# Talking-heads attention with a bilinear MoE: six q times k of a chunk begun one unit later, and loads of k, v, x and weights at other units

## The chip, the cores and the metric

One core of one Trainium2 chip runs the whole program. The metric is device time in microseconds (us), the median of several executions; in a profiled execution the span from the core's first to its last instruction is also known.

## The reference

```python
scores = scale * np.matmul(q, k.transpose(0, 1, 3, 2))        # batch 4, heads 12, seq 448, dim 64
scores = np.einsum('bhij,hg->bgij', scores, w_pre)            # heads are mixed
scores = scores - np.max(scores, axis=-1, keepdims=True)
attn = np.exp(scores)
attn = attn / (np.sum(attn, axis=-1, keepdims=True) + 1e-09)
attn = np.einsum('bhij,hg->bgij', attn, w_post)               # and mixed again
x = np.matmul(attn, v)                                        # then laid out as 1792 x 768
a, b = x @ w_a, x @ w_b                                       # 768 -> 1536
out = (a * b) @ w_out                                         # 1536 -> 768
```

## The kernel before

Attention runs first, the MoE after it. A batch has 448 queries, cut into four chunks of 120, 120, 120 and 88, and each chunk into units of 20 queries (the last of a batch has 8). That makes 16 chunks and 92 units, 23 to a batch. The main loop runs over the units s, and everything is written out in the order in which each engine gets it; there is no scheduler behind it.

For a whole chunk, six calls of `qk(c, i)` multiply q by k for two heads each, into one PSUM tile of two banks, `pst`, of which there is one. The result is copied to the scores `s` in SBUF, by ACT for i = 0 and 3 (`i % OWN == 0`), by DVE for the others. There are two tiles of `s`, so chunk c writes where chunk c - 2 was. `gather(u)`, four DMAs issued by POOL (`sb<-s`), brings the rows of a unit into `sb`, with all heads of a few queries side by side. It is issued AH = 4 units before use, and the first of a chunk only once all six `qk` have been issued.

A unit s then does this: `premix(s)` (PE: `mp<-sb,wp`, heads mixed); `evac_p(s - 2)` (ACT: `pt<-pp`); `smax(s)` (DVE: `nm`, the row maximum; ACT: `a`, the exponential with its row sum); the items of the table `items`, that is `qk` of a coming chunk and `av` (PE: `xp<-pt,v`, attention times v, at odd units of a batch mostly, one or two calls); `norm(s)` (DVE: `rs`, `rc`, `kr`); `postmix(s - 1)` (PE: `pp<-kr,a`, the second mixing and a transposition). Of two `qk` in one unit, the second is issued after `postmix`; such a unit is said to have a pair. At the end of a unit stand loads of k and q (table `after`).

In `items`, chunk c's six `qk` begin at the unit a = starts[c - 1] - 4 and are spread evenly up to starts[c] - 5; starts[c] is the chunk's first unit. Counted in the batch, that is units 2 to 7 for the second chunk, 8 to 13 for the third, 14 (a pair) to 18 for the next batch's first, 19 to 22, 0 and 1 for its second. Chunk 1 has a table of its own.

Loads are issued by SP. Batch 0's v comes in 12 pieces, two a unit, from unit V_FIRST; the next batch's v comes one piece a unit from unit V_AT of a batch on; the next batch's six pieces of k every other unit from K_AT. At unit `last_prep + 1` (83) the tiles of q and k are given up, and the first two blocks of MoE weights (`raw`, three pieces each) and the six parts of x (`xhl`) are loaded; `tail` is the work that splits them, a few steps a unit.

Of the kernel before, what the change touches and what calls it, by code (L numbers as in the profile page):

```python
# [21 lines left out]
def talking_heads_bilinear_kernel(  # L22
# [12 lines left out]
    B, _, G, S = k.shape  # L35
# [26 lines left out]
    WARM = 40  # L62
    WARM3 = 60
    Q1E = 3
    V_AT = 8
    V_FIRST = 1
    V_PIECES = 12
    K_AT = 3
    OWN = 3
    LQ = 4  # L70
    scale = 1.0 / float(D) ** 0.5
# [2 lines left out]
    for b in range(B):  # L74
        t0 = 0
        while t0 < S:
            n = min(CHUNK, S - t0)
# [8 lines left out]
    NUB = NU // B  # L86
# [40 lines left out]
    def later(fn, n=3):  # L127
        todo_at.setdefault(now[0] + n, []).append(fn)
# [62 lines left out]
    def load_v(b, i):  # L191
        g, i = divmod(i, V_PIECES // 2)
        e, i = divmod(i, V_PIECES // 4)
        n = H // 2 // (V_PIECES // 4)
        rows, heads = slice(64 * e, 64 * e + C), slice(n * i, n * i + n)
        nc.sync.dma_start(out=vt[b % 2][g][rows, heads], in_=v[b, g][C * e:C * e + C, heads])
# [199 lines left out]
    items, after, ready = {}, {}, {}  # L396
    starts = [u for u in range(NU) if units[u][1] == 0] + [NU]
    qk_at = {}
    for c in range(1, NC):
        b, t0, _ = chunks[c]  # L400
        a, e = max(starts[c - 1] - AH, 0), starts[c] - AH
        for i in range(G):
            at_s = qk_at[c, i] = i * Q1E // G if c == 1 else a + i * (e - a) // G
            items.setdefault(at_s, []).append((qk, c, i))
            if t0 == 0:
                after.setdefault((b - 1) * NUB + K_AT + 2 * i, []).append((load_k, b, i))
        ready[c] = qk_at[c, G - 1]
        for j in range(G // QG):
            if c > 1:
                when = max(qk_at[c, QG * j] - LQ, 0)  # L410
                after.setdefault(when, []).insert(0, (load_q, c, j))
            if c > 1 or j:
                after.setdefault(max(qk_at[c, QG * j] - 1, 0), []).append((spread_q, c, j))
    last_prep = ready[NC - 1]
    for a in range(NA - 1):
        b, u0, n = groups[a]
# [6 lines left out]
    def open_moe():  # L423
        short.close()
        mo["c"] = ctx.enter_context(tc.tile_pool(name="mc", bufs=2))
        mo["w"] = ctx.enter_context(tc.tile_pool(name="mw", bufs=2))
# [16 lines left out]
    def load_raw(u, parts=1):  # L443
        kind, i, e = u
        t = mo["c"].tile([128, CW, 2], I32, tag="raw", name="raw")
        to, src = t.rearrange("p (k f) t -> p k (f t)", k=KD), (w_ab if kind == "f" else w_out)[i, e].bitcast(I32)
        n = KD // parts
        raws[u] = t
        return [
            lambda k=k: nc.sync.dma_start(out=to[:, k:k + n], in_=src[:, k:k + n]) for k in range(0, KD, n)  # L450
        ]
# [166 lines left out]
    with tc.manual_schedule():  # L618
# [30 lines left out]
        for s in range(NU + 2):  # L649
            now[0] = s  # L650
            if s == last_prep + 1:
                open_moe()
                pieces = load_raw(order[0], 3) + load_raw(order[1], 3)
                pieces += [lambda i=i: load_x(0, (i,)) for i in range(KD)]
                for i, fn in enumerate(pieces):
                    fn() if i < 3 else later(fn, (i - 1) // 2)
                tail = tail_ops()
            if s == NU - 2:
                load_x(1)
            if s == NU - 1:  # L660
                load_x(2)
            while nxt_g <= min(s + AH, NU - 1) and ready.get(units[nxt_g][0], -1) < s:
                gather(nxt_g)
                nxt_g += 1
            b, i = divmod(s, NUB)
            if 0 <= s - V_FIRST < V_PIECES // 2:
                for p in range(2):
                    load_v(0, 2 * (s - V_FIRST) + p)
            if b + 1 < B and 0 <= i - V_AT < V_PIECES:
                load_v(b + 1, i - V_AT)  # L670
            for fn in todo_at.pop(s, ()):
                fn()
            if s < NU:
                premix(s)
            if 2 <= s <= NU:
                evac_p(s - 2)
            if s < NU:
                for k_ in blocks_of(s):
                    smax(k_)
            pairs = [it for it in items.get(s, ()) if it[0] is qk]  # L680
            for it in items.get(s, ()):
                if it not in pairs[1:]:
                    it[0](*it[1:])
            if s < NU:
                norm(s)
            if 0 <= s - 1 < NU:
                postmix(s - 1)
            for it in pairs[1:]:
                it[0](*it[1:])
            for it in after.get(s, ()):  # L690
                it[0](*it[1:])
            if s >= last_prep + 2:
                take(tail, RATE if s < NU - LATE else RATE2)
            if s == NU:
                for _ in tail:
                    pass
                tail = split_ops(1)
                evac_p(NU - 1)
                run_a(0, 0)
            if s == NU + 1:  # L700
                run_b(0, 0)
# [59 lines left out]
        for j in range(B * KD):  # L761
            b, m = divmod(j, KD)
# [57 lines left out]
```

## Time and profile before

| | |
|---|---|
| median of 3 runs | 927.26 us (924.5 to 930.05) |
| the profiled execution | 927.72 us, of which its span is 926.0 us |
| mean granted clock of TensorE | 0.983 of full speed |
| PE busy | 881.8 us, 95% of the span |
| DVE, ACT, POOL busy | 520.6, 365.6, 444.7 us |
| DMA, mean over the span | 159 GB/s |

The difference of 1.7 us between the execution and its span lies before the first and behind the last instruction. Attention takes about the first 382 us. The busy share of PE is a mean over that part, in which it waits at times, and the MoE, in which it hardly ever does.

### The profile page before, as it was taken

The page shows a single profiled execution, that of the slowest core. Times are in us where ns is not written, and L with a number is a line of the kernel's source. Part 1 is how long each engine was busy: PE and PEld are TensorE (multiplying, and loading weights), DVE is VectorE, ACT ScalarE, POOL GpSimd, SP SyncE. Part 2 cuts the span into 40 slices and gives each one's busy share as a digit, 9 for nine tenths or more (in the row PEclk, how much of TensorE's full clock was granted, in tenths as well). Part 3 has the DMA queues.
Part 4 walks back from the last instruction along what each step waited for, and adds up shares of the span by engine and source line. Part 5 has one row for each costly group of instructions (what it writes and reads, how often), then busy time and mean ns, then how long its engine had stood idle before and what let it go on. Part 6 is the DMA issues. An engine that isn't in the chain of part 4 may idle for free.

```text
span 926.0 us, 26343 instructions
## 1 busy us (share of the span) xinstructions
PE 881.8 (95%) x11092; PEld 709.0 (77%) x11092; DVE 520.6 (56%) x899; ACT 365.6 (39%) x841; POOL 444.7 (48%) x551
## 2 busy tenths in 40 slices
PE   7879998899899997899999999999999999999998
PEld 4445665566566664788999999999999989999997
DVE  4656776767667767477755755557455445151500
ACT  1556676667656775522111111111111244343531
POOL 7466676766757764033333322233232245554552
PEclk9789999999999998999999999999999999999999
DMA  5598667855966567543533333342342664746441
GB/s 157 163 200 173 172 178 182 198 157 163 217 148 172 163 173 190 183 140 123 167 119 145 108 137 128 116 149 98 118 147 92 233 231 148 256 132 252 132 146 60
DMA packets 78647, 147.40 MB, mean 159 GB/s; under 512 B 29342, under 2 KB 58122, under 8 KB 77506
## 3 DMA queue, kind: packets, MB, share of 16 engines
q1 hardware_dynamic: 50402, 108.05, 36.4%
q0 software_dynamic: 28128, 37.68, 16.2%
q8 instruction: 87, 1.43, 0.7%
q14 instruction: 30, 0.25, 0.1%
HBM read 80.23 MB, written 26.74 MB: 116 GB/s over the span
## 4 chain that ended last, share of the span: by engine, by line
PE 70%; POOL 7%; DMA 7%; DVE 6%; issue 6%; ACT 3%; SPq 0%; ACTq 0%; DVEq 0%; POOLq 0%
PE po L510 6%; PE po L511 6%; PE po L509 6%; PE pa L509 6%; PE pa L511 6%; PE pb L511 6%; PE pa L510 6%; PE pb L509 6%; PE pb L510 6%; POOL sb L285 5%; DMA sb<-s 5%; PE xp L384 4%; PE pst L241 4%; PE pp L348 4%; PE mp L305 4%
## 5 line engine op out<-in xcount | busy, mean ns | idle before, releaser
L285 POOL DMA_DIRECT2D sb<-s x350 | 201.3, 584 | 105.3 <-PE mp L305 30.1
L471 POOL TENSOR_TENSOR cvm<-cvm,cvr 128x768 int32<-128x768 int32 x36 | 66.9, 1858 | 224.3 <-DVE cvm L470 219.2
L499 POOL TENSOR_TENSOR wl<-rawo,wh 128x768 fp32r<-128x768 f32 x48 | 93.2, 1962 | 105.2 <-ACT wh L498 105.2
L315 DVE TENSOR_REDUCE nm<-mp 124x1 f32<-124x448 f32 x180 | 104.0, 617 | 69.0 <-PE mp L305 63.5
L318 ACT ACTIVATE a<-mp,nm 124x448 f32<-124x448 f32 x180 | 112.9, 634 | 70.6 <-DVE nm L315 70.5
L348 PEld LDWEIGHTS pp<-kr,a 60*56 60x56 f32 (+1 forms) x5760 | 98.0, 129 | 45.1 <-issue 29.7
L521 ACT COPY sa<-pa 128x448 f32<-128x448 f32 x48 | 25.6, 533 | 232.7 <-PE pa L511 171.2
L241 PE MATMUL pst<-k,q 64*64 64x448 f32 (+1 forms) x744 | 100.7, 580 | 16.0 <-ACT s L268 11.8
L348 PE MATMUL pp<-kr,a 60*56 60x60 f32 (+1 forms) x5760 | 102.1, 217 | 14.4 <-issue 10.7
L363 ACT COPY pt<-pp 120x480 f32<-120x480 f32 x176 | 91.1, 576 | 53.9 <-PE pp L348 53.5
L305 PE MATMUL mp<-sb,wp 60*64 60x448 f32 x720 | 102.9, 565 | 5.3 <-DMA sb<-s 2.6
L510 PE MATMUL pa<-xhl,wh 128*128 128x448 f32 x288 | 104.8, 364 | 1.7 <-DVE xhl L439 1.7
L510 PE MATMUL po<-hl,wh 128*128 128x448 f32 x288 | 105.8, 367 | 0.6 <-DVE hl L546 0.6
L509 PE MATMUL pa<-xhl,wh 128*128 128x448 f32 x288 | 106.0, 368 | 0.0
L511 PE MATMUL pa<-xhl,wl 128*128 128x448 f32 x288 | 105.9, 368 | 0.0
L511 PE MATMUL po<-hh,wl 128*128 128x448 f32 x288 | 105.8, 368 | 0.0
L509 PE MATMUL po<-hh,wh 128*128 128x448 f32 x288 | 105.1, 365 | 0.0
L511 PE MATMUL pb<-xhl,wl 128*128 128x448 f32 x282 | 103.8, 368 | 0.7 <-POOL wl L499 0.7
L531 DVE TENSOR_TENSOR hf<-pb,sa 128x448 f32<-128x448 f32 x47 | 29.3, 624 | 133.4 <-PE pb L511 123.7
L509 PE MATMUL pb<-xhl,wh 128*128 128x448 f32 x282 | 103.6, 367 | 0.0
L510 PE MATMUL pb<-xhl,wh 128*128 128x448 f32 x282 | 102.4, 363 | 0.0
L546 DVE TENSOR_TENSOR hl<-hl,hh 128x448 fp32r<-128x448 f32 x48 | 57.3, 1248 | 78.5 <-ACT hh L545 78.5
(74 smaller groups left out, 1343.0 us busy)
## 6 DMA issues: line engine op xcount, KB each, us to landing
sb<-s POOLq DMA_DIRECT2D x346, 105.0 KB, 4.6
rawo<-wod SPq DMA_DIRECT2D x24, 768.0 KB
raw<-in_w_ab_dram SPq DMA_DIRECT2D x22, 768.0 KB
hd<-hf SPq DMA_DIRECT2D x48, 224.0 KB
raw<-in_w_out_dram SPq DMA_DIRECT2D x12, 768.0 KB
k<-in_k_dram SPq DMA_DIRECT2D x24, 224.0 KB
v<-in_v_dram SPq DMA_DIRECT2D x48, 112.0 KB
xhl<-xd SPq DMA_DIRECT2D x24, 224.0 KB
```

The source lines that it names most:

```text
L241: nc.tensor.matmul(out[64 * e:64 * e + cols.stop - cols.start], lhsT=qt[c, i // QG][rows, i % QG, cols], rhs=kt[b, i][rows],)
L285: (nc.sync if u <= AH and i % 2 else nc.gpsimd).dma_start(out=sbt[u][i % 2][r:r + m * H], in_=rows)
L305: nc.tensor.matmul(mt[u, i // 2][col:col + M], lhsT=wp[r:r + m, :M], rhs=tiles[i % 2][r:r + m])
L315: nc.vector.tensor_reduce(nm[:m], mp[:m], axis=AXX, op=ALU.max, negate=True)
L318: nc.scalar.activation(a[:m], mp[:m], ACTF.Exp, bias=nm[:m], scale=1.0, accum_out=rss[u][:m, j:j + 1])
L348: nc.tensor.matmul(pp_t[i][64 * e:64 * e + C, H * r:H * r + H, j, :m], lhsT=a[rows, keys:keys + C], rhs=kr[rows, j, :, :m],)
L363: nc.scalar.copy(to[:C2, :, o + QB * i:o + QB * i + QB], pp_t[i][:C2].rearrange("p x j t -> p x (j t)"))
L471: lambda: nc.gpsimd.tensor_tensor(m, m, r, op=ALU.add),
L499: nc.gpsimd.tensor_tensor(ll[:, sl], raw, hh.bitcast(F32)[:, sl], op=ALU.subtract)
L509: nc.tensor.matmul(o, lhsT=hh[:, k0 + kk], rhs=mh[:, kk], start=(kk == 0), stop=False)
L510: nc.tensor.matmul(o, lhsT=hh[:, k0 + kk], rhs=ml[:, kk], start=False, stop=False)
L511: nc.tensor.matmul(o, lhsT=ll[:, k0 + kk], rhs=mh[:, kk], start=False, stop=(kk == n - 1))
```

## The change

The starts of `qk` move: a chunk with six units gets its six `qk` at a + 1, a + 2, a + 3 (two), a + 4, a + 5, one with five units (the next batch's first) at a + 1, a + 2 (two), a + 3, a + 4 (two). So the last one stays at its unit. In a batch the second chunk's are now at units 3, 4, 5 (two), 6, 7, the third's at 9, 10, 11 (two), 12, 13, the next batch's first at 15, 16 (two), 17, 18 (two), its second's at 20, 21, 22 (two), 0, 1. Units 2, 8, 14 and 19 have none. Loads of k and v get a table of units each; batch 0's v starts one unit later; the MoE's first loads get a table too, and the tail's steps begin one unit later.

```diff
@@ -62,10 +62,11 @@
     WARM = 40
     WARM3 = 60
     Q1E = 3
-    V_AT = 8
-    V_FIRST = 1
+    V_FIRST = 2
     V_PIECES = 12
-    K_AT = 3
+    V_UNITS = (8, 11, 13, 15, 15, 17, 17, 19, 19, 21, 21, 22)
+    K_UNITS = (2, 3, 6, 9, 10, 14)
+    M_UNITS = (0, 0, 1, 1, 2, 3, 3, 4, 4, 5, 5, 5)
     OWN = 3
     LQ = 4
     scale = 1.0 / float(D) ** 0.5
@@ -400,10 +401,10 @@
         b, t0, _ = chunks[c]
         a, e = max(starts[c - 1] - AH, 0), starts[c] - AH
         for i in range(G):
-            at_s = qk_at[c, i] = i * Q1E // G if c == 1 else a + i * (e - a) // G
+            at_s = qk_at[c, i] = i * Q1E // G if c == 1 else a + 1 + (i * (e - a - 1) + 2) // G
             items.setdefault(at_s, []).append((qk, c, i))
             if t0 == 0:
-                after.setdefault((b - 1) * NUB + K_AT + 2 * i, []).append((load_k, b, i))
+                after.setdefault((b - 1) * NUB + K_UNITS[i], []).append((load_k, b, i))
         ready[c] = qk_at[c, G - 1]
         for j in range(G // QG):
             if c > 1:
@@ -652,8 +653,8 @@
                 open_moe()
                 pieces = load_raw(order[0], 3) + load_raw(order[1], 3)
                 pieces += [lambda i=i: load_x(0, (i,)) for i in range(KD)]
-                for i, fn in enumerate(pieces):
-                    fn() if i < 3 else later(fn, (i - 1) // 2)
+                for fn, n in zip(pieces, M_UNITS):
+                    later(fn, n)
                 tail = tail_ops()
             if s == NU - 2:
                 load_x(1)
@@ -666,8 +667,9 @@
             if 0 <= s - V_FIRST < V_PIECES // 2:
                 for p in range(2):
                     load_v(0, 2 * (s - V_FIRST) + p)
-            if b + 1 < B and 0 <= i - V_AT < V_PIECES:
-                load_v(b + 1, i - V_AT)
+            for p in range(V_PIECES):
+                if b + 1 < B and i == V_UNITS[p]:
+                    load_v(b + 1, p)
             for fn in todo_at.pop(s, ()):
                 fn()
             if s < NU:
@@ -689,7 +691,7 @@
                 it[0](*it[1:])
             for it in after.get(s, ()):
                 it[0](*it[1:])
-            if s >= last_prep + 2:
+            if s >= last_prep + 3:
                 take(tail, RATE if s < NU - LATE else RATE2)
             if s == NU:
                 for _ in tail:
```

DVE, batch 0, from unit 14 on, before: `nm` opens a unit, `rs`, `rc`, `kr` are its `norm`, each `COPY s<-pst` evicts one q times k (unit 14's first is ACT's).

```order
L315 TENSOR_REDUCE nm<-mp 124x1 x2
L328 TENSOR_SCALAR rs<-rs 124x2
L329 RECIPROCAL rc<-rs 124x2
L331 TENSOR_TENSOR kr<-kf,rc 124x120
L266 COPY s<-pst 124x2x448
L315 TENSOR_REDUCE nm<-mp 124x1 x2
L266 COPY s<-pst 124x2x448
```

Two units further, in the changed kernel, from unit 16 on:

```order
L316 TENSOR_REDUCE nm<-mp 124x1 x2
L267 COPY s<-pst 124x2x448
L329 TENSOR_SCALAR rs<-rs 124x2
L330 RECIPROCAL rc<-rs 124x2
L332 TENSOR_TENSOR kr<-kf,rc 124x120
L267 COPY s<-pst 124x2x448
L316 TENSOR_REDUCE nm<-mp 124x1 x2
```

The pair has gone from unit 14, where ACT evicted its first half, to unit 16, where DVE evicts both, one ahead of `norm` and one behind it.

ACT, batch 1, units 2 and 3, before: `a` is the exponential of a unit, `pt` the eviction of postmix two units back, `s<-pst` the eviction of the chunk's first q times k.

```order
L318 ACTIVATE a,rs<-mp,nm 124x448 x2
L268 COPY s<-pst 124x2x448
L363 COPY pt<-pp_101 120x48x10
L363 COPY pt<-pp_102 120x48x10
L318 ACTIVATE a,rs<-mp,nm 124x448 x2
```

The same place in the changed kernel:

```order
L319 ACTIVATE a,rs<-mp,nm 124x448 x2
L364 COPY pt<-pp_101 120x48x10
L364 COPY pt<-pp_102 120x48x10
L319 ACTIVATE a,rs<-mp,nm 124x448 x2
L269 COPY s<-pst 124x2x448
```

The eviction of q times k has moved from behind unit 2's exponentials to behind unit 3's.

SP, batch 1, from unit 9's load of k on, before: `paced` is a small write that each unit issues when its first maximum is there, so the rows between two of them belong to the end of one unit and the start of the next.

```order
L203 DMA k<-in_k_dram 128x448
L196 DMA v_103<-in_v_dram 56x512
L199 DMA paced<-nm 1x1
L210 DMA qraw<-in_q_dram 128x360
L196 DMA v_103<-in_v_dram 56x512
L199 DMA paced<-nm 1x1
L203 DMA k<-in_k_dram 128x448
L196 DMA v_103<-in_v_dram 56x512
L394 DMA xd_85<-xs 128x3x160
```

From unit 9's load of k on in the changed kernel:

```order
L204 DMA k<-in_k_dram 128x448
L200 DMA paced<-nm 1x1
L204 DMA k<-in_k_dram 128x448
L197 DMA v_103<-in_v_dram 56x512
L200 DMA paced<-nm 1x1
L211 DMA qraw<-in_q_dram 128x360
L395 DMA xd_85<-xs 128x3x160
L200 DMA paced<-nm 1x1
L197 DMA v_103<-in_v_dram 56x512
```

Before, units 9 to 12 hold two loads of k and three of v; now k stands at the ends of units 9 and 10, and v in units 11 and 13.

## Rows read from the trace of the kernel before

**Rows 1.** Stretches: length, busy time by engine, PE clock, DMA share, GB/s.

```profile
56.52:84.33 27.81, 24.91 (x579) 15.94 (x574) 15.47 (x35) 15.47 (x38) 18.48 (x38) 0.88 0.80 185
...
146.84:170.23 23.39, 21.50 (x577) 14.46 (x568) 15.70 (x39) 15.53 (x38) 16.59 (x32) 1.00 0.87 216
170.23:203.82 33.59, 31.21 (x834) 20.20 (x826) 22.05 (x49) 22.56 (x55) 22.34 (x41) 1.00 0.68 166
232.25:258.16 25.91, 23.19 (x577) 15.07 (x568) 15.85 (x39) 15.64 (x38) 17.87 (x36) 0.93 0.98 214
...
319.40:341.28 21.88, 21.45 (x576) 14.42 (x568) 15.68 (x39) 15.40 (x38) 15.95 (x31) 1.00 0.55 170
341.28:381.62 40.34, 32.11 (x804) 20.42 (x792) 28.93 (x65) 25.18 (x62) 17.37 (x20) 0.92 0.74 196
```

**Rows 2.** Waits of PE in 17 to 382 us: total, times, longest.

```profile
PE pst L241 <- ACT s L268: 11.5, 15, 2.5
PE pp L348 <- issue: 10.7, 7, 2.9
```

**Rows 3.** Timeline of PE, batch 0, units 9 and 10: start, us, instruction, [idle].

```profile
60.90 0.54 PE L305 MATMUL mp<-sb,wp 60*64 60x448 f32 x1
...
64.35 1.77 PE L241 MATMUL pst<-k,q 64*64 64x448 f32 x8 [2.46 <-ACT s L268]
...
70.03 0.94 PE L305 MATMUL mp<-sb,wp 60*64 60x448 f32 x8
```

**Rows 4.** Timeline of ACT at the same place.

```profile
63.39 0.91 ACT L268 COPY s<-pst 107x896 f32<-107x896 f32 x1 [3.73 <-DMA sb<-s]
```

**Rows 5.** Timeline of PE, batch 0, units 2 and 3.

```profile
36.96 1.76 PE L241 MATMUL pst<-k,q 64*64 64x448 f32 x8 [1.31 <-DVE s L266]
38.47 1.74 PE L305 MATMUL mp<-sb,wp 60*64 60x448 f32 x8
```

**Rows 6.** Timeline of PE, batch 1, units 14 to 22.

```profile
170.23 0.94 PE L305 MATMUL mp<-sb,wp 60*64 60x448 f32 x8
...
174.24 0.98 PE L241 MATMUL pst<-k,q 64*64 64x448 f32 x8 [1.48 <-ACT s L268]
175.04 0.93 PE L305 MATMUL mp<-sb,wp 60*64 60x448 f32 x8
176.44 0.98 PE L241 MATMUL pst<-k,q 64*64 64x448 f32 x8 [0.46 <-DVE s L266]
...
181.82 1.16 PE L305 MATMUL mp<-sb,wp 60*64 60x448 f32 x8
183.41 0.98 PE L241 MATMUL pst<-k,q 64*64 64x448 f32 x8 [0.43 <-ACT s L268]
...
187.56 0.94 PE L305 MATMUL mp<-sb,wp 60*64 60x448 f32 x8
...
194.12 0.94 PE L305 MATMUL mp<-sb,wp 60*64 60x448 f32 x8
...
196.47 1.16 PE L305 MATMUL mp<-sb,wp 60*64 60x448 f32 x8
...
201.53 0.55 PE L305 MATMUL mp<-sb,wp 60*64 60x448 f32 x2
```

**Rows 7.** Timeline of DVE, batch 1, unit 14.

```profile
171.27 1.16 DVE L315 TENSOR_REDUCE nm<-mp 124x1 f32<-124x448 f32 x2 [1.77 <-PE mp L305]
```

**Rows 8.** Timeline of ACT, batch 1, unit 14.

```profile
173.28 0.91 ACT L268 COPY s<-pst 124x896 f32<-124x896 f32 x1
```

**Rows 9.** Timeline of PE, batch 3, units 14 to 16.

```profile
341.28 0.94 PE L305 MATMUL mp<-sb,wp 60*64 60x448 f32 x8
...
343.43 0.56 PE L305 MATMUL mp<-sb,wp 60*64 60x448 f32 x1
...
351.43 0.86 PE L348 MATMUL pp<-kr,a 60*56 60x60 f32 x24 [2.85 <-issue]
```

**Rows 10.** Timeline of PE, batch 2, unit 12.

```profile
251.53 0.27 PE L348 MATMUL pp<-kr,a 60*56 60x60 f32 x3 [1.91 <-issue]
```

## Prediction

> **What bounds the kernel now.** I read the stretches first, cut at the premix matmul that opens a unit; i is a unit's number in its batch, 0 to 22. TensorE (PE) is the engine that is nearly always busy: in the undisturbed stretch for units 8 to 13 of the last batch it works 21.45 of 21.88 us. The same six units take 27.81, 23.39 and 25.91 us in the three batches before, where the DMA share is 0.80 to 0.98 instead of 0.55 and in two of them the clock is below 1.00 [rows 1]. So some 11.5 us (5.9, 1.5 and 4.0) are lost there, the only large losses between the start and the last nine units. Units 14 to 22 show none: 31.21 of 33.59 us at a share of 0.68.
>
> The waits of PE come next. Besides waits for the eviction of q times k (ACT alone 11.5 us), seven waits of pp, 10.7 us, are put down to "issue": PE waited for nothing that the profile shows [rows 2]. The longest, 2.85 us, lies in the last stretch, at a share of 0.74 and a clock of 0.92 [rows 1, 9].
>
> The timeline at the start of batch 0's last chunk shows what the first edit is about. ACT idles 3.73 us for a gather that still reads the old scores (sb<-s) and evicts at 63.39 [rows 4]. The next unit's q times k needs the one PSUM tile pst, so PE waits 2.46 us and then runs its eight matmuls at half speed (1.77 us for 0.98), and the unit from 60.90 to 70.03 takes 9.13 us [rows 3]. A unit of the same kind, with a double attention-times-v, takes 5.06 (196.47 to 201.53) [rows 6].
>
> **The change, part by part.** No instruction is added or taken away. What a q times k costs depends on the unit that it stands in, and units alternate: even ones have no attention times v, odd ones a single or double one. Prices from PE's starts:
> - an even unit with one q times k: 2.35 (194.12 to 196.47) [rows 6]; without one: 2.15 (341.28 to 343.43) [rows 9], since postmix, its eviction and the next postmix still follow each other. Taking one away returns 0.2, not its 0.9 of matmul.
> - an even unit with a pair: 4.81 (170.23 to 175.04), 1.48 of it the wait for the first eviction, and 0.46 more in the next unit for the second [rows 6]. ACT began that first eviction only at 173.28, behind its exponentials [rows 8]; DVE would be free after its reduces, at 172.43 [rows 7], 0.8 sooner. So a pair with DVE first is 4.1, or +1.75 over one.
> - an odd unit is PE's own pace: one more q times k is +0.9, and the next unit gets about 0.5 more, since ACT evicts it ahead of the postmix result (no row shows this; between 0 and the 0.98 of matmul and 0.9 of eviction, I take the 0.46 of [rows 6]).
> - after an even unit whose q times k ACT evicts, the next pays 0.43; with a double attention times v it is 5.74 (181.82 to 187.56) instead of 5.06: 0.7 [rows 6].
>
> *The later start.* Units 2 to 13: 2 and 8 lose their q times k (-0.2 each), 3 and 9 lose the ACT stall (-0.4, -0.7), 5 and 11 take a pair (+0.9 each), 6 and 12 follow it (+0.5 each): +1.3 a batch, +3.9 for three. Batch 0 has no attention times v in unit 5, so its pair is of the even kind: 1.75 + 0.5 - 0.2 + 0.9 + 0.5 = +3.45; its units 2, 3 and 9 are priced below. Units 14 to 22 and the next 0 (three times): 14 loses its pair, 4.81 to 2.15, -2.65; 15 loses 0.46 of stall; 16 and 18 get pairs with DVE first, +1.75 each; 17 keeps a stall, -0.3; 19 loses its one, -0.75 (0.9 less a little of the 2.15 effect); 21 gets the 0.7; 22, with only eight queries, takes a pair at +1.3 (between the 0.9 of matmul and 1.75), 0 the +0.5. Together +1.85, +5.6 for three. In all **+13.0 us**. Its ends are 6 (pairs at their matmuls alone) and 19 (every new even pair as dear as the ACT one, +2.46).
>
> What the move takes away: in unit 2 of batch 0 the third q times k waits 1.31 and starts at 36.96; without it the next premix, at 38.47, could start at 35.65 [rows 5]: **-2.8**. Unit 9 of batch 0 falls from 9.13 to 5.06: **-4.1**. The gather that ended that wait landed at about 63.3 [rows 4]; with q times k one unit later, ACT comes to this eviction at about that time, so the wait is covered. If unit 2's gain brings PE there earlier, the gather, which is queued behind the same premixes, comes earlier too, or up to 2.8 of the wait stays.
>
> *The loads.* Six pieces of v and three of k lie in units 8 to 13 now, three and two after. By their shapes a piece of k has 128 x 448 x 4 bytes = 224 KB and one of v 112 KB, so that is 784 KB instead of 1344, 42% less of the loads that make 0.80 to 0.98 of 0.55. That puts the three stretches at about 0.70 to 0.80; at 0.68 [rows 1] nothing was lost. The excess goes steeply with the share (1.5 us at 0.87, 4.0 at 0.98). The pieces that go to units 14 to 22, three more of 112 KB over 33 us, raise 0.68 by a few hundredths. They bound a small loss, one wait of the mean size 1.5 a batch; I take nothing. SP's queue issues the same transfers in another order, behind the same small paced writes, and k and v keep several units of lead.
>
> What is there to get: the excess without unit 9's part, 1.8 + 1.5 + 4.0 = 7.3. Two of the seven issue waits lie in these stretches, one of 1.91 us in the third [rows 10]; the other five, at the mean of 10.7 / 7, make 7.6. Clock in the last stretch: 0.92 over 40.34 us is 6.5 us at 1.2 GHz, at most 3.2 lost; 1.6 as the half that follows such a wait. Sum 16.5. The ends are 0 and 16.5; I take three quarters, nearest to the 0.68 row, **-12.4**.
>
> *Issue waits and the Trainium skill.* The rows say that PE stood 10.7 us with nothing to wait for, and the 1.91 and the 2.85 of them lie where the DMA share was 0.98 and 0.74 [rows 1, 2, 9, 10]. The Trainium skill, "Runtime: NRT & Kernel Launch", section on instruction fetch mechanics, says that engines fetch their instructions in 16 KiB blocks through a DMA queue and that this is mostly hidden behind issue. By that page these waits would not be fetches held up by loads, moving loads would leave them, and the sum would lose its last term (rival 1). The waits of [rows 2] are not hidden, so I hold with the row.
>
> *MoE loads and the tail.* First weights and x are issued a little more spread, the tail's DVE work starts one unit later, four of its steps pass to the second-last units. That work had ended before the first MoE matmul needed it, with a unit to spare, so I add nothing; the last stretch has 40.34 us for nine units [rows 1], and if the delay shows at its end it costs up to one unit, 4.
>
> **Sum**, against the profiled execution's own 927.7 (span 926.0; the median shown is 927.3, so no correction): 927.7 + 13.0 - 2.8 - 4.1 - 12.4 = **921.4**, 0.7% less.
>
> **Rivals.**
> 1. *The loads are relieved, but PE's waits stay.* They do not hang on the load, or return wherever PE's program has few instructions at hand; only the price of the pairs is then left: 927.7 + 13.0 - 6.9 = 933.8. It ends slower by over 0.5% once relief returns less than 1.5 us. For it: one could take "issue" at its word. Against: three stretches lose in the order of their DMA share [rows 1].
> 2. *Half the relief*, because batch 0's first units stay as full of v and k as they were (v of batch 0 only moves by a unit) and the tail's waits fall anew: 927.7 + 13.0 - 6.9 - 8.2 = 925.6, no change that can be told.
> 3. *The change does not do what it says:* the gather of unit 11 still ends the eviction's wait. Then 4.1 shrinks to about 1.3 and the sum is 924.2, again no change to speak of.
> 4. *Cheap pairs:* the evictions that I price as stalls fall into time that PE loses anyway, the cost is 6, and all relief comes: 927.7 + 6 - 6.9 - 16.5 = 910.3.
>
> **How the numbers follow.** A difference under 0.5% (4.6 us) is about what a measurement of this kernel can't tell from none. Forecast 0.40, rival 4 0.12: faster 0.52. Rivals 2 and 3, 0.20 and 0.10: same 0.30. Rival 1, 0.18: slower. The range goes from rival 4 to rival 1, 911 to 933, which leaves out the outer part of each; the forecast's own range is 916 to 926, from five eighths to all of the relief and 2 us of pair price either way.
>
> **What would show it.** Right: units 8 to 13 at 23 to 25 us in each of the first three batches with a DMA share under 0.85; units 14 to 22 some 2 us longer than 33.59; unit 9 of batch 0 near 5; the seven issue waits down to two or three; waits of q times k on evictions up by several us, on DVE's above all. Wrong: issue waits as long as before (rival 1), units 14 to 22 no longer than now (rival 4 in its price), a double-length wait of ACT for sb<-s in batch 0 (rival 3). Most of all the sum rests on two terms of about 13 us with opposite signs, and a third of either is enough to move the verdict.

## The result, and the profile after

The changed kernel takes 934.6 us in the median (928.8 to 937.8, 19 runs), the kernel before 926.6 us beside it (922.7 to 930.1, 19 runs): a ratio of 1.0076 with a 95% interval of 1.0058 to 1.0095, 0.8% slower. The profiled execution took 931.9 us, 2.7 below its median, with a span of 930.2 us for 926.0 and a clock of 0.989 for 0.983. All 19 runs lie above the own range of the forecast (916 to 926), and the median above the whole range.

The stretches of the changed kernel that answer to [rows 1]: units 8 to 13 of batches 0, 1, 2 and 3, and units 14 to 22 of batches 1 and 2.

```profile
52.97:82.57 29.60, 24.89 (x579) 15.83 (x571) 16.49 (x39) 16.32 (x42) 19.45 (x40) 0.88 0.73 175
148.68:171.06 22.38, 21.97 (x576) 14.38 (x568) 15.55 (x39) 15.44 (x38) 16.91 (x35) 1.00 0.73 196
171.06:206.66 35.60, 31.79 (x835) 20.54 (x828) 22.74 (x52) 22.70 (x55) 22.37 (x41) 1.00 0.70 162
235.69:259.19 23.50, 21.94 (x577) 14.87 (x566) 15.80 (x39) 15.58 (x38) 16.95 (x35) 1.00 0.71 191
259.19:295.52 36.33, 32.45 (x835) 20.73 (x828) 22.38 (x52) 22.73 (x55) 23.33 (x43) 1.00 0.68 161
324.99:347.34 22.35, 21.93 (x577) 14.29 (x568) 15.56 (x39) 15.45 (x38) 16.90 (x35) 1.00 0.52 164
```

Three things are to be seen. In batches 1 and 2 units 8 to 13 are shorter by 1.0 and 2.4 us, and the DMA share has gone from 0.87 and 0.98 to 0.73 and 0.71. Units 14 to 22 are longer by 2.0 us in batch 1, by 3.0 in batch 2 (36.33, and 33.35 from 258.16 to 291.51 before) and by 3.7 in batch 0 (37.18 from 82.57 on, and 33.50 from 84.33 before). Batch 0's stretch, which was to shrink, has grown from 27.81 to 29.60 at the same clock of 0.88.

The waits of PE answer to [rows 2], in the same window (total, times, longest).

```profile
PE pst L242 <- POOL q L225: 7.9, 5, 3.1
PE pst L242 <- DVE s L267: 6.7, 9, 1.7
PE pst L242 <- POOL q L231: 4.0, 1, 4.0
PE pst L242 <- ACT s L269: 4.0, 12, 1.0
PE mp L306 <- ACT a L319: 3.6, 2, 3.1
PE pp L349 <- issue: 3.5, 4, 1.9
```

Issue waits fell from 10.7 to 3.5 us and waits for ACT's evictions from 11.5 to 4.0. But at the head stands a waiter that cost 0.2 us before: POOL, 7.9 and 4.0, together 11.9 us, for `q`. This is what `spread_q` writes, the copy that brings the loaded q into the order that `qk` reads.

PE in units 9 and 10 of batch 0, which answers to [rows 3].

```profile
55.63 0.54 PE L306 MATMUL mp<-sb,wp 60*64 60x448 f32 x1
...
60.96 1.88 PE L242 MATMUL pst<-k,q 64*64 64x448 f32 x8 [3.99 <-POOL q L231]
62.77 4.05 PE L385 MATMUL xp<-pt,v 120*64 120x160 f32 x32
66.75 1.06 PE L349 MATMUL pp<-kr,a 60*56 60x60 f32 x64
67.64 0.63 PE L306 MATMUL mp<-sb,wp 60*64 60x448 f32 x4
```

POOL at the same place, where `sb<-s` are the gathers and L225, L231 and L233 one `spread_q`.

```profile
56.90 0.58 POOL L286 DMA_DIRECT2D sb<-s  x1 [0.90 <-PE mp L306]
57.97 0.57 POOL L286 DMA_DIRECT2D sb<-s  x1 [0.49 <-DMA sb<-s]
59.49 0.57 POOL L286 DMA_DIRECT2D sb<-s  x1 [0.95 <-DMA sb<-s]
60.06 0.71 POOL L225 COPY q<-qraw 128x120 f32<-128x120 f32 x2
60.71 0.19 POOL L231 COPY q<-qraw 128x15 f32<-128x15 f32 x1
60.85 0.18 POOL L233 COPY q<-qraw 128x9 f32<-128x9 f32 x1
```

The copies stand behind gathers that wait, for a tile which PE has yet to read and for transfers, and they start only when the last of these is out, at 60.06. PE's q times k follows at 60.96, after 3.99 us, and both its eight matmuls (1.88) and the attention times v behind them (4.05, for 2.39 at full clock) run at the lower of the two clock levels. The unit lasts 12.01 us, from 55.63 to 67.64. The Trainium skill, "Perfetto Trace Analysis", section on per-instruction lifecycle, says that ACT, DVE and GpSimd execute strictly in the order of their queue; these rows agree.

ACT at the same place, which answers to [rows 4].

```profile
62.99 0.91 ACT L269 COPY s<-pst 107x896 f32<-107x896 f32 x1 [3.74 <-DMA sb<-s]
```

The label is that of before, almost to the hundredth. But the matmuls that this copy reads ended at 62.84 (60.96 and 1.88), so PE's lateness alone explains its start.

### The profile page after: what moved, and what is told of

Its sections match the earlier page's. It is cut to its first block, busy times and chain, and to the rows that moved or that the text cites. A ratio compares the mean times of both kernels' runs of the same rounds, so it can differ in the third digit from the quotient of the medians.

```text
span 930.2 us, 26369 instructions
## 1 busy us (share of the span) xinstructions
PE 879.7 (95%) x11092; PEld 707.3 (76%) x11092; DVE 521.1 (56%) x899; ACT 365.3 (39%) x841; POOL 447.3 (48%) x551
## 4 chain that ended last, share of the span: by engine, by line
PE 74%; issue 8%; POOL 5%; DMA 5%; DVE 4%; ACT 3%; SPq 0%; DVEq 0%; ACTq 0%; POOLq 0%
PE po L511 6%; PE po L512 6%; PE po L510 6%; PE pa L510 6%; PE pa L512 6%; PE pa L511 6%; PE pb L512 6%; PE pb L510 6%; PE pb L511 6%; PE pst L242 6%; PE xp L385 5%; PE pp L349 5%; POOL sb L286 4%; PE mp L306 4%; DMA sb<-s 3%
## 5 line engine op out<-in xcount | busy, mean ns | idle before, releaser
L286 POOL DMA_DIRECT2D sb<-s x350 | 201.6, 590 | 113.2 <-issue 33.7
L349 PEld LDWEIGHTS pp<-kr,a 60*56 60x56 f32 x5760 | 94.9, 128 | 44.6 <-ACT pt L364 22.8
L349 PE MATMUL pp<-kr,a 60*56 60x60 f32 x5760 | 104.0, 216 | 9.2 <-issue 3.5
```

What stands on the lines that cost most here:

```text
L286: (nc.sync if u <= AH and i % 2 else nc.gpsimd).dma_start(out=sbt[u][i % 2][r:r + m * H], in_=rows)
L349: nc.tensor.matmul(pp_t[i][64 * e:64 * e + C, H * r:H * r + H, j, :m], lhsT=a[rows, keys:keys + C], rhs=kr[rows, j, :, :m],)
```

## The experiments

The theory after the two traces: the edit of one index moved not only `qk` but, through `qk_at`, the `spread_q` that stands a unit ahead of it. Before, the spread for a chunk's first three `qk` stood on POOL ahead of the first gather of the chunk in front of it; now it stands behind that gather, which waits for the last eviction of its own chunk and for free tiles. The rivals: the loads' new places cost; the pairs cost by themselves; the relief of the loads is less than predicted. All times, with the kernel before run beside each:

| kernel | median us (runs) | before us | ratio, 95% interval |
|---|---|---|---|
| e1 starts only | 933.9 (6) | 926.7 | 1.0098 [1.0066, 1.0130] |
| e2 all loads only | 927.4 (12) | 926.7 | 1.0008 [0.9980, 1.0037] |
| e3 changed, spread early | 925.9 (12) | 926.7 | 1.0004 [0.9984, 1.0025] |
| e4 k and v only | 926.3 (12) | 926.7 | 0.9997 [0.9972, 1.0022] |
| e5 two chunks, changed loads | 920.5 (7) | 926.5 | 0.9946 [0.9923, 0.9970] |
| e6 two chunks, old loads | 925.6 (12) | 926.5 | 0.9993 [0.9973, 1.0013] |
| e7 no k and v after batch 0 | 917.7 (6) | 926.5 | 0.9908 [0.9887, 0.9928] |
| e8 spread early in batch 0 | 929.7 (12) | 926.5 | 1.0028 [1.0005, 1.0052] |
| e9 e5 without the MoE part | 922.4 (12) | 927.3 | 0.9944 [0.9920, 0.9967] |
| e10 e9, batch 3 as before | 920.9 (12) | 927.3 | 0.9933 [0.9911, 0.9955] |
| e11 other chunks, old loads | 937.8 (9) | 927.3 | 1.0098 [1.0064, 1.0132] |
| e12 e9, loads out of 8 to 13 | 919.4 (6) | 927.3 | 0.9910 [0.9875, 0.9946] |
| e13 changed, spread on DVE | 937.0 (6) | 924.9 | 1.0127 [1.0094, 1.0159] |
| e14 e12, batch 3 as before | 921.0 (9) | 924.9 | 0.9949 [0.9922, 0.9975] |
| e15 batch 0's chunks only | 919.2 (6) | 924.9 | 0.9934 [0.9909, 0.9959] |
| e16 loads out, old starts | 923.7 (12) | 924.9 | 0.9990 [0.9969, 1.0011] |

Differences in us between kernels of different rows are worked out below from the ratios, as a share of 927 us; each is uncertain by about 3 us.

### The two halves of the change

e1 is the kernel before with one line of the change:

```diff
-            at_s = qk_at[c, i] = i * Q1E // G if c == 1 else a + i * (e - a) // G
+            at_s = qk_at[c, i] = i * Q1E // G if c == 1 else a + 1 + (i * (e - a - 1) + 2) // G
```

> The kernel before with the later starts of q times k alone; all loads as before. Theory (the later start puts spread_q behind the first gather of a chunk on POOL's queue, and PE waits for the q that it writes): the waits of PE for POOL's q are there as in the changed kernel, some 12 us in all (3 to 4 us in units 5 and 9 of batch 0, 1.4 us in unit 20 of each batch), and the time is above both kernels, 936 to 941 us. Rival a (the loss comes from the new places of the loads, the starts cost nothing): 924 to 929 us, no different from before. Rival b (the pairs' price of 13.0 us of the prediction, without POOL): as slow, 936 to 940 us, but then the waits of PE are put down to DVE's and ACT's evictions and not to POOL.

e2 is the changed kernel with that line put back; e4 has in addition the MoE's pieces and the tail as before:

```diff
-                for fn, n in zip(pieces, M_UNITS):
-                    later(fn, n)
+                for i, fn in enumerate(pieces):
+                    fn() if i < 3 else later(fn, (i - 1) // 2)
...
-            if s >= last_prep + 3:
+            if s >= last_prep + 2:
```

> The changed kernel with the starts of q times k as before; the loads of k, v, the MoE's first pieces and the tail's delay as in the change. Theory (the loads relieve, the starts cost): no wait of PE for POOL's q over 0.5 us, the pp waits on issue at 3 to 5 us in place of 10.7, units 8 to 13 of batches 1 and 2 shorter by 1 to 2.5 us, and 917 to 922 us, faster than both. Rival a (the places of the loads are what costs): 930 us or more. Rival c (the relief comes only together with the later starts): 925 to 928 us.

> The kernel before with the new places of the loads of k and v alone (batch 0's v one unit later among them); starts of q times k, the MoE's first pieces and the tail as before. If the relief of 12.4 us is in the loads of k and v: 917 to 922 us, with units 8 to 13 of batches 1 and 2 shorter by 1 to 2.5 us each and a DMA share there under 0.85. If the MoE's pieces and the tail's delay carry part of it, this kernel is slower than the one with all loads by that part (up to 3 us, from the clock of the last nine units).

The whole loss is in the starts: e1 is 9 us slower (0.98%), the changed kernel 7 (0.76%), so the loads return 2 us there by the two ratios, which can't be told from nothing. Alone they return nothing that can be told: e2 and e4 stand at 1.0008 and 0.9997. Here the theory's 917 to 922 was missed, and the time is in rival c's range. e1's 933.9 lies between what the theory and rival a asked for, and in its profile PE waits 6.6 us for POOL's `q` at one line and 1.1 at the other, 4 less than expected. Another expectation for e2 was missed too: with the starts as before, its profile still has waits for POOL's `q` of 2.6 and 1.4 us, in batch 0, where none over 0.5 was expected. So the move of the copies is not the only thing that can make `q` late.

### POOL's order

e3 is the changed kernel with the spread one unit earlier, ahead of that gather again, and its load as well:

```diff
-    LQ = 4
+    LQ = 5
...
-                after.setdefault(max(qk_at[c, QG * j] - 1, 0), []).append((spread_q, c, j))
+                after.setdefault(max(qk_at[c, QG * j] - 2, 0), []).append((spread_q, c, j))
```

> The changed kernel, with q loaded and spread one unit earlier, so that the spread_q of a chunk's first half stands ahead of the first gather on POOL again; starts of q times k and all loads of k, v and the MoE as in the change. Theory: PE's waits for POOL's q (11.9 us) go, and what of the half clock in batch 0 follows them; part of the 4 us in unit 9 returns as a wait for the eviction that ACT makes, which waits for a gather. 921 to 926 us. Rival b (PE would have waited there anyway for evictions or gathers): 932 to 936 us, as the changed kernel, with the same waits under other names.

e8 does that for batch 0's chunks alone (1 less where `c < 4`, in both lines).

> The changed kernel with q spread one unit earlier for batch 0's chunks alone; in batches 1 to 3 POOL's order and the 1.4 us waits for q in unit 20 stay. If the cost of the change lies in batch 0 (waits of 3.1 and 4.0 us and the half clock behind them): 925 to 928 us, as with all chunks spread earlier. If the waits of 1.4 and 0.6 us in the later batches (4.8 us) count as well: 929 to 931 us.

e3 took 925.9 us: 0.72% less than the changed kernel, 6.7 us, by the copies of q, and the loads that they read, one unit earlier. That the loads alone would have done it is not likely: in the changed kernel's trace POOL starts the copies for units 5, 9 and 20 at the moment at which the gather ahead of them ends (59.49 and 0.57 make 60.06), so they waited for no load. In e3's profile a single wait for POOL's `q` is left, 0.76 us, and unit 9 of batch 0, from 55.05 to 62.76, has lost the half clock:

```profile
55.05 0.54 PE L306 MATMUL mp<-sb,wp 60*64 60x448 f32 x1
...
58.53 1.09 PE L242 MATMUL pst<-k,q 64*64 64x448 f32 x8 [0.76 <-POOL q L231]
59.55 2.39 PE L385 MATMUL xp<-pt,v 120*64 120x160 f32 x32
61.88 1.06 PE L349 MATMUL pp<-kr,a 60*56 60x60 f32 x64
62.76 0.63 PE L306 MATMUL mp<-sb,wp 60*64 60x448 f32 x4
```

e8 lies between: two thirds of the 6.7 us are batch 0's (0.48%, 4.4 us). The rest, 2.2 us, can't be told from nothing by the ratios. What e8 leaves are the waits of 1.4 us in unit 20 of the first three batches, where q of the next batch is spread, and one of 0.6 us. The one of batch 2 in the changed kernel:

```profile
285.21 0.98 PE L242 MATMUL pst<-k,q 64*64 64x448 f32 x8 [1.41 <-POOL q L225]
```

Such a wait costs less than its length, since unit 21 is then shorter: in batch 2 units 20 and 21 take 8.89 us together in the changed kernel and 8.06 in e3.

The wait of 3.1 us, in unit 5 of batch 0, is of another kind. PE and POOL there, first before, then changed:

```profile
45.65 0.98 PE L241 MATMUL pst<-k,q 64*64 64x448 f32 x8 [0.20 <-DVE rs L328]
44.64 0.96 POOL L224 COPY q<-qraw 128x180 f32<-128x180 f32 x2
...
45.75 1.77 PE L242 MATMUL pst<-k,q 64*64 64x448 f32 x8 [3.10 <-POOL q L225]
44.77 0.93 POOL L225 COPY q<-qraw 128x180 f32<-128x180 f32 x2
```

These copies belong to the chunk's fourth q times k, whose unit the change leaves as it was, and POOL makes them at the same time in both traces. What moved is PE: it opens unit 5 at 40.04 instead of 44.15 and then waits, and unit 6 begins at 47.30 in both. So `q` that was not moved took back here what PE had gained up to unit 5. e3 and e8 put these copies a unit earlier too; their gain is therefore more than the change's own displacement undone.

e13 leaves the place and changes the engine:

```diff
-                after.setdefault(max(qk_at[c, QG * j] - 1, 0), []).append((spread_q, c, j))
+                after.setdefault(max(qk_at[c, QG * j] - 1, 0), []).append((spread_q, c, j, nc.vector))
```

> The changed kernel with every later spread of q on DVE at the same place in the program; POOL issues gathers alone. Starts and loads as in the change. Theory (q is late because its copies stand in POOL's queue behind gathers that wait): the waits for POOL's q are gone, waits for q from DVE stay under 0.5 us each, and the time falls to 924 to 930 us, though DVE has some 30 us more to do and evicts q times k a little later. Rival (one unit is too short a lead on any engine): PE waits 3 to 4 us for DVE's q in units 5 and 9 of batch 0, and 933 us or more.

The time, 937.0 us, is the rival's, but its waits are not there. No wait for `q` is longer than 1.1 us, and unit 9 of batch 0 is down to 6.32 us (57.87 to 64.19) with

```profile
60.01 1.04 PE L242 MATMUL pst<-k,q 64*64 64x448 f32 x8 [0.85 <-DVE q L231]
```

so with one unit's lead `q` is late by under 1.1 us there instead of 4. But with DVE, which also evicts most q times k, PE waits a little wherever a spread stands, where under 0.5 us each was expected. It is 12.1 us in 14 waits, as much as the 11.9 for POOL:

```profile
PE pst L242 <- DVE q L225: 8.7, 10, 1.1
...
PE pst L242 <- DVE q L231: 3.4, 4, 0.9
```

As a whole it isn't a cure, and by its time alone it would have spoken against the theory. It shows that the long waits come from POOL's queue, and not that the loss does; for that e3 and e8 stand.

### What the starts are worth, chunk by chunk

e5 moves only the two chunks of a batch whose q times k run in units 2 to 13, with their q spread a unit earlier; e6 is the same with all loads as before. (The section on the kernel before and the expectations call them the second and third chunk. Counted from a batch's first, they are its third and fourth, as `c % 4 > 1` says; the second is the one in units 19 to 1.)

```diff
+            at_s = qk_at[c, i] = i * Q1E // G if c == 1 else a + 1 + (i * (e - a - 1) + 2) // G if c % 4 > 1 else a + i * (e - a) // G
...
+                when = max(qk_at[c, QG * j] - LQ - (c % 4 > 1), 0)
...
+                after.setdefault(max(qk_at[c, QG * j] - 1 - (c % 4 > 1), 0), []).append((spread_q, c, j))
```

> Later starts, with q spread one unit earlier, for the second and third chunk of each batch alone (the q times k of units 2 to 13); the chunks whose q times k run in units 14 to 1 start as before; loads as in the change. Theory (the later start pays in units 2 to 13 once POOL's order is mended, and costs 2 to 3 us a batch in units 14 to 22, where it stays): batch 0 to unit 14 shorter than before by 4 to 6 us, units 14 to 22 back at 33.5 to 34.3 us, 916 to 921 us. Rival (what the starts give in units 2 to 13 is scatter of single profiles): 924 to 928 us.

> The same starts and the same spread of q as in the kernel with two chunks moved, with all loads as in the kernel before. If the new places of the loads give nothing (as the kernel with the loads alone, 927.4 us beside 926.7, had it): within 2 us of that kernel. If they give relief only together with the later starts: 3 us or more above it.

e11 is the complement of e6: `c % 4 < 2` (chunk 1 excepted) in the place of `c % 4 > 1`.

> The kernel before with the later starts for the other chunks alone, those whose q times k run in units 14 to 1, their q spread one unit earlier so that POOL's order stays; all loads as before. It prices the pairs by themselves. By the prediction's term: +5.6 us for units 14 to 22 (35.4 us each in place of 33.5), 931 to 933 us. By what the profiles with POOL's waits show (35.6 to 37.2 us) less those waits: +4 to +8 us. Rival (the pairs cost nothing once POOL's order is right): 926 to 928 us.

e9 is e5 with e4's lines on the MoE; e10 is e9 with `1 < c % 4 and c < 12`, e15 e9 with `1 < c < 4`, in the place of `c % 4 > 1`.

> The kernel with two chunks moved (920.5 us, loads as in the change) with the MoE's first pieces and the tail's delay put back as before. In the profiles with the tail's delay the last nine units take 37.6 to 38.6 us, with a wait of 3.7 us of mp for ACT's exponential in unit 88, and without it some 36. If that is the delay's price: 917.5 to 919.5 us, and the last nine units near 36. If it is scatter: 920 to 921 us.

> The same kernel, with the two chunks of batch 3 starting as before. Batch 3 has no loads of a next batch, so the later start has nothing to relieve there; profiles with it show units 69 to 82 at 50.7 us, without it 49.8. Theory (the later start pays only beside crowded DMA): 0.5 to 1.5 us below the kernel that moves them in all batches. Rival (it pays everywhere alike): 1 us or more above it.

> Later starts for the second and third chunk of batch 0 alone, with q spread a unit earlier there; all else as in the kernel before but for the change's places of k and v. If the gain of some 5 us of the two-chunk kernels is batch 0's (units 2 and 9): 920.5 to 923 us. If half of it is in batches 1 and 2 (units 8 to 13 at 22.5 and 22.8 us for 23.4 and 25.9): 923 to 925 us.

One index, and three different prices. The chunks of units 14 to 1 cost 9 us by themselves (e11, [5.9, 12.2]), above every range expected, although no wait for POOL's `q` is left in its profile; but that profile is of its fastest execution, 930.0 us. With the changed loads it is 5.4 (e3 less e5). The two chunks of units 2 to 13 give 5 us back with the changed loads (e5 and e9). And e15 has all of that gain in batch 0 alone: 6.1 us ([3.8, 8.4]). In batches 1 to 3 the later start in units 2 to 13 shows no gain or loss in the time that can be told. The traces show a small loss in batch 3, which loads no k and v for a next batch: units 2 to 13 take 41.76 us with the old starts (e15, 292.52 to 334.28) and 42.73 with the later ones (e5, 290.72 to 333.45). The stretches of e15, units 2 to 4 and 8 to 13 of batch 0, then 8 to 13 of batches 1 and 2, whose starts are as before:

```profile
31.01:41.12 10.11, 8.99 (x249) 4.73 (x244) 7.38 (x15) 7.95 (x19) 4.67 (x9) 1.00 0.57 166
53.50:79.30 25.80, 23.63 (x579) 14.57 (x573) 15.35 (x35) 15.63 (x38) 20.50 (x41) 1.00 0.83 193
140.76:164.45 23.69, 21.93 (x576) 14.30 (x568) 16.32 (x40) 15.79 (x40) 17.30 (x33) 1.00 0.68 189
...
227.01:250.29 23.28, 21.51 (x575) 14.50 (x568) 16.11 (x39) 15.62 (x38) 17.33 (x35) 1.00 0.77 196
```

From the start of unit 2 to that of unit 14 of batch 0 e15 takes 48.29 us (31.01 to 79.30), where the kernel before takes 53.38 and the changed one 54.15 (28.42 to 82.57). The same two sums of before, units 2 to 4 and 2 to 13:

```profile
30.95:44.15 13.20, 11.11 (x258) 5.58 (x253) 7.65 (x16) 7.72 (x17) 7.33 (x14) 0.87 0.55 165
30.95:84.33 53.38, 44.95 (x1060) 26.82 (x1056) 32.07 (x71) 31.67 (x77) 33.71 (x65) 0.90 0.79 184
```

Of the 5.1 us some 3.1 are in units 2 to 4 and 2.0 in units 8 to 13, and the mean clock of both stretches has gone to 1.00. How it is shared out between them is one profile's: with the later starts units 2 to 4 take from 10.1 us (e15) to 13.3 (e1), and unit 2 itself begins between 28.3 and 31.4.

e9 and e5 differ by the MoE's pieces and the tail alone, and stand at 0.9944 and 0.9946: these edits cost nothing that can be told.

### What the loads can give

e7 is the kernel before without the loads of k and v of batches 1 to 3, which use batch 0's:

```diff
     def load_v(b, i):
+        if b:
+            return
...
-                    lhsT=vt[b % 2][g][:C2, h % G, r],
+                    lhsT=vt[0][g][:C2, h % G, r],
...
     def load_k(b, i):
+        if b:
+            kt[b, i] = kt[0, i]
+            return
```

> The kernel before without any load of k and v for batches 1 to 3 (these batches use batch 0's k and v in its place, so part of the result is another). It bounds what any placing of these loads can give. By the prediction's term (7 to 12 us of lost time hang on the DMA load): units 8 to 13 at 22 us in all of the first three batches, pp waits on issue down to 1 or 2 us, 915 to 920 us. By the theory after the first runs (the losses do not come from these loads): 923 to 927 us, with pp waits on issue still at 5 us or more.

The time, 917.7 us, is what the prediction's term asked for and not what the theory did: 8.5 us less ([6.7, 10.5]). The loads do cost. Of PE's waits on issue one is left, where pp alone had 10.7 us:

```profile
PE mp L310 <- issue: 0.4, 1, 0.4
```

One profile doesn't tie these waits to the loads, though. e2 and e9 have all loads, those of k and v at the changed places, and their rows are

```profile
PE pp L349 <- issue: 8.4, 9, 1.5
...
PE pp L349 <- issue: 0.9, 2, 0.7
```

What ends such a wait the traces do show. The larger of the two DMA queues named instruction moves packets of 16,384 bytes, 65 of them between 17 and 382 us in the kernel before. Each of the seven waits of pp there ends 1.24 to 1.63 us after one of them has landed. So do, 1.23 to 1.97 us after, all 80 such waits of 0.3 us or more in the traces of all kernels, though only 13 of 100 moments taken at random lie that near. So they are most likely waits for the next piece of PE's program; no run moved those packets, and why some come late stays open.

In e7 batch 0 keeps its knot, with the starts as before and a DMA share of 0.53 (units 8 to 13):

```profile
51.85:80.40 28.55, 24.50 (x579) 15.91 (x571) 17.52 (x39) 16.51 (x42) 19.88 (x40) 0.88 0.53 150
```

Its wait is now for POOL: `pst` for `q` L235, once, 4.1 us, in unit 8.

e12 and e16 don't drop the loads of k and v but take them out of units 8 to 13, except for one piece of k; e12 on e9, e16 with all starts as before. e14 is e12 with e10's condition. The lines in which e12 differs from e9:

```diff
-    V_UNITS = (8, 11, 13, 15, 15, 17, 17, 19, 19, 21, 21, 22)
-    K_UNITS = (2, 3, 6, 9, 10, 14)
+    V_UNITS = (14, 14, 15, 16, 16, 17, 18, 18, 19, 20, 21, 22)
+    K_UNITS = (1, 3, 5, 7, 11, 14)
```

> The kernel with two chunks moved and the MoE's pieces as before, with all twelve loads of v moved to units 14 to 22 and those of k to units 1, 3, 5, 7, 11 and 14, so that units 8 to 13 hold one load of 224 KB in place of five. If the loss in units 8 to 13 hangs on the loads that lie there: 1 to 2 us below the same kernel with the change's places, with units 14 to 22 no longer than 34 us. If it hangs on the gathers' own traffic, or if units 14 to 22 pay: the same or slower.

> Later starts for the second and third chunk of batches 0 to 2, q spread a unit earlier, loads of v in units 14 to 22 and k as in the kernel with the loads out; the MoE's pieces as before. If the gains of emptier units 8 to 13 and of leaving batch 3 alone are real and add up: 916 to 919 us, the fastest with the whole work done. If each was scatter: 920 to 922 us.

> The kernel before with v loaded in units 14 to 22 and k in units 1, 3, 5, 7, 11 and 14; starts as before. Leaving all loads of k and v out gave 8.7 us with the starts as before, the change's places gave none. If loads in units 8 to 13 are what costs: 919 to 923 us, with units 8 to 13 of batches 1 and 2 near 22 us. If the loss comes back wherever the loads stand, or needs the later starts to be relieved: 925 us or more.

e16's profile is one of a kernel without a fault in batches 1 and 2, 21.87 us in both for units 8 to 13, as in the undisturbed batch 3 of [rows 1]:

```profile
144.25:166.12 21.87, 21.43 (x577) 14.18 (x568) 15.60 (x39) 15.42 (x38) 16.77 (x32) 1.00 0.66 192
...
228.36:250.23 21.87, 21.43 (x576) 14.18 (x568) 16.07 (x39) 15.46 (x38) 16.68 (x34) 1.00 0.75 201
```

But that was its fastest execution (918.8 us); the median is 923.7, by the interval between 2.9 us less and 1.0 more than before. And in batch 0 it has the longest wait of all for POOL:

```profile
58.63 1.88 PE L242 MATMUL pst<-k,q 64*64 64x448 f32 x8 [5.33 <-POOL q L231]
```

The fastest kernels that do the whole work, e5, e9, e10, e12, e14 and e15, lie between 0.9910 and 0.9949 with overlapping intervals; e12 has the lowest ratio, but which of them is best can't be told. The expectations for e9, e10 and e12 turned on 1 to 3 us and stay undecided. That emptier units 8 to 13 and leaving batch 3 alone add up (e14's expectation) did not show.

## Why the prediction was wrong

The sum came out 13 us too low. The step that failed by most is the last of "The loads": "three quarters, nearest to the 0.68 row, -12.4". The moved loads gave nothing alone (e2, e4, e16) and 2 us, not to be told from none, in the changed kernel. Taking the loads of batches 1 to 3 away altogether is worth 8.5 us with the starts as before, so moving them could hardly give 12.4. The signs named for it came all the same: issue waits at 3.5 us, a DMA share of 0.73 and 0.71, units 8 to 13 of batches 1 and 2 shorter. They were not signs of it: e1, with the old loads, has 23.02 and 23.19 us there, at shares of 0.82 and 0.81. The mistake was to count three quarters of what one profiled execution had lost as something that another place of the load returns. The single profiles of kernels with moved loads show issue waits of pp from 0.9 us (e9) to 8.4 (e2), and the medians don't follow them. Two readings behind the term were wrong as well. The three stretches do not lose in the order of their DMA share, as rival 1 has it: the one at 0.80 loses most, 5.9 us, and more than the one at 0.87 even without unit 9. And units 14 to 22 get a piece of k beside the three of v, 560 KB and not 336.

The second failed step is in "What the move takes away": "Unit 9 of batch 0 falls from 9.13 to 5.06: -4.1", with "the wait is covered". It rose to 12.01, and the cause is a row that the sum doesn't have. The part follows each moved matmul and eviction through PE, ACT and DVE, but `spread_q`, whose unit is derived from `qk_at`, moves as well, past a gather on POOL's queue. With `q` spread earlier than in the change, 6.7 us come back (e3), part of them in unit 5, where the copies had not moved. In its place the prediction put 0. That the eviction's own wait would be covered did come true once `q` was there: in e3 ACT idles 3.66 us and evicts at 62.91, and PE's next q times k, at 63.87, doesn't wait for it.

With that order mended, the prediction's view of batch 0 holds in its sign. It had 3.45 for the pairs there less 2.8 and 4.1 for units 2 and 9, together -3.5; e15, which moves these chunks alone (and k and v to the places of the change, worth nothing by e4), gains 6.1. Units 2 to 4 are 3.1 us shorter in its profile, near the -2.8. In the changed kernel PE opens unit 5 4.1 us earlier than before and loses that again there, to a copy that the sum doesn't have either. Unit 9 only partly follows: in the kernels that spread q early it takes from 5.37 us (e6, 57.23 to 62.61) to 9.05 (e9, 54.51 to 63.56), where 5.06 was expected. What holds PE up in units 8 and 9 of batch 0 is whoever comes last, ACT's eviction for 2.46 us in [rows 3], POOL's `q` for 4.1 in e7, 5.33 in e16 and 3.99 in the changed kernel. Rival 3's sign, ACT's idle time of 3.74 us, came true without deciding: PE itself was late.

The price of the pairs by unit was good: an even unit without q times k takes 2.11 us (259.19 to 261.30) for 2.15, a pair with DVE first 4.05 (275.83 to 279.88) for 4.1. What units 14 to 22 cost as a whole, 9 us in e11 and 5 between e3 and e5, was forecast as 5.6. Unit by unit the traces bear the 5.6 out: taken where nothing disturbs them, units 14 to 22 come to 34.8 us with the later starts and `q` in time (e3, e11) and to 33.3 with the old (e5), and the unit behind them takes 3.81 for 3.58, so 1.7 us a batch for the 1.85 forecast. What e11's one profile has beyond that are single disturbances, such as an issue wait of 2.26 us in unit 16 of batch 1. For units 2 to 13 of batches 1 to 3 the +3.9 was not seen in the time: e15, which leaves them out, and e9 differ by 0.1%, 0.9 us; in batch 3's rows it is 1.0 for the 1.3.

The MoE's edits were costed at nothing, and e5 and e9 show nothing. Rival 1 has the right time, 933.8, by another mechanism: the waits it takes to stay fell to a third, and new ones on POOL took their place. The Trainium skill, "Runtime: NRT & Kernel Launch", section on instruction fetch mechanics, calls fetches mostly hidden. The trace before agrees, with seven waits of pp to 65 packets. But it does not follow, as the prediction read it, that these waits are no fetches held up: each ends shortly after such a packet has landed.

What stays open: why the new places of the loads are worth 4.4 us between e6 and e5, with the starts moved in two chunks, and nothing with the starts as before; and why the other chunks cost 9 us with the old loads. Single profiles scatter too much to find either. With the old loads it is not shown, either, that POOL's order matters: e11, which keeps it, and e1, which doesn't, stand at the same ratio, and all starts moved with the old loads and `q` spread early was not run.

## What to carry to other kernels

When a table of places is edited, list everything that is derived from it, and follow each instruction along its own queue: here a small copy that moved past a DMA issue inherited all that the DMA waited for. Look also at what has not moved: where an engine gets faster, a copy that was just in time is late. Take the size of a contention from an experiment without the traffic before crediting a move of it, and count only a part, since traffic that is moved still has to pass. A wait label names the releaser that came last; look whether the producer itself had just ended before the label is believed.

## What had not been expected of the hardware

A wait of PE can cost more than its length. In the changed kernel the clock fell to the lower of its two levels, 1.2 GHz, within the wait of 3.99 us and stayed there until 5.2 us after PE's work had resumed at 60.96, and the 32 matmuls of one attention times v took 4.05 us for 2.39. The stretches ahead of the fall, at the lower level and behind it:

```profile
56.97:59.40 2.43, 0.00 (x1) 0.00 (x0) 1.47 (x4) 1.84 (x6) 1.08 (x2) 0.99 0.96 174
59.40:66.20 6.80, 5.24 (x34) 3.48 (x36) 0.65 (x3) 0.91 (x1) 5.96 (x13) 0.50 0.63 163
66.20:67.64 1.44, 1.44 (x75) 1.22 (x72) 0.00 (x0) 0.00 (x0) 1.17 (x5) 1.00 0.51 173
```

Issuing the gathers keeps POOL busy by itself. In the changed kernel it is 350 issues of 590 ns on average, 201.6 us, and beside them 113.2 us idle just ahead of them:

```profile
L286 POOL DMA_DIRECT2D sb<-s x350 | 201.6, 590 | 113.2 <-issue 33.7
```

The copies of q that shared this queue came as late as the gathers ahead of them.
